# Attention forward and backward with grouped heads: K, V, dV and dK in nine shared places, and another order of the first three iterations

## The chip, the cores and the metric

The kernel runs on one core of one Trainium2 chip. The metric is the device time of one execution in microseconds (us): the median of three runs before the change is 684.23 us, the lowest 682.85, the highest 688.73. A core has these engines, each with its own instruction queue: TensorE (PE in the profile; its weight loads are PEld), VectorE (DVE), ScalarE (ACT), GpSimd (POOL) and SyncE (SP). Sixteen DMA engines move data between the device memory and the on-chip memory; in this kernel SP and POOL issue the transfers.

## The reference

For each of 32 batch entries there are 32 query heads with 4 queries each, 4 key/value heads with 2048 keys each, and a width of 128. Eight query heads share one key/value head. The forward pass and its gradients are wanted:

```python
k = jnp.repeat(k, rep, axis=1)          # rep = 32 // 4
v = jnp.repeat(v, rep, axis=1)
scores = jnp.einsum("bhqd,bhkd->bhqk", q, k) * D ** -0.5
p = softmax(scores, axis=-1)
out = jnp.einsum("bhqk,bhkd->bhqd", p, v)
# outputs: out, and the gradients of it for q, k, v with grad_out
```

All tensors are bf16. K, V, dK and dV are 2 MB each per batch entry, all else is small, so the kernel reads 136.31 MB and writes 136.31 MB.

## The kernel before

One iteration is one batch entry `b`. Its 32 x 4 = 128 query rows fill the 128 partitions: 32 rows (`G`) for each of 4 key/value heads (`NH`). The 2048 keys of a head are laid out as 128 partitions x 16 blocks (`C`), so K, V, dK and dV of one entry are each one tile of 128 partitions x 4 heads x 16 blocks x 128 numbers, 16 KB in each partition.

The work of an entry is cut into named pieces. `LK` and `LV` (lines 144 and 155) load K and V, one DMA of 512 KB for each head, issued by SP; every fourth `LK` also has the next four entries' q and grad_out loaded (`GROUP`). `QDT` transposes q and grad_out on TensorE; `KT0` to `KT7` and `VT0` to `VT7` transpose eight blocks of K or V each (eight matmuls against an identity, line 180) and VectorE copies the result out of PSUM (line 182). `Sa` and `Sb` are the scores of one half of the keys each (line 197) with the row maximum on VectorE (line 210); `EXa` and `EXb` are the exponentials on ScalarE (line 221). `NRM` makes the reciprocal sums on VectorE and, on GpSimd, the scaled query rows `dop` and `qp` (line 230). `ETa`, `ETb` transpose the exponentials (line 247). `O` multiplies them with V (line 263), and from the output comes the row term `delta`. `dPa`, `dPb` give `ds` (line 349), `dSTa`, `dSTb` transpose it, and `dQ` multiplies it with K (line 263). `dV0` to `dV7` and `dK0` to `dK7` are the outer products (line 306), two blocks of all heads each, copied out of PSUM by ScalarE (line 310). When all eight parts of a dV or dK are there, it is stored (line 132), by GpSimd until the last V has been asked for, then by SP; most stores are one DMA of 2 MB, dV of entry 0 and of every fourth entry is cut into three.

The order of all this is written out by hand. Inside `tc.manual_schedule()` (line 373) the pieces are emitted one after the other: `HEAD` for the first three iterations, `STEADY` (48 pieces, `+` and `-` marking a later or an earlier entry) for the iterations in the middle, `TAIL` for the last three. Each engine works through its own queue in that order, and an instruction waits on semaphores for what it needs. PSUM is one tile of eight banks, handed out by the class `Banks`, the bank released longest ago first.

The on-chip places of the four large tensors come from three pools: three buffers for K (`k_pool`, line 92), two for V (`v_pool`), four shared in turn by dV and dK (`out_pool`, line 100). A pool gives its buffers in rotation. So the load of K of entry b waits until `dQ` of entry b-3 has read the buffer, the load of V until `O` of entry b-2 has, and the first copy into a dV or dK until the store of the fourth output before it has landed.

Of the kernel before, what the change touches and what calls it, by code (L numbers as in the profile page):

```python
# [14 lines left out]


HEAD = """
LK@0 LV@0 QDT@0 KT4@0 KT6@0 KT2@0 KT0@0 KT3@0 KT5@0 KT1@0 KT7@0 LK@1 LV@1 VT2@0 Sa@0 Sb@0 VT5@0 VT3@0 EXb@0 VT4@0 EXa@0 VT0@0 QDT@1 KT4@1
KT6@1 KT2@1 KT0@1 NRM@0 ETb@0 ETa@0 VT7@0 KT3@1 VT6@0 VT1@0 dV7@0 O@0 dV5@0 dPb@0 dV1@0 KT5@1 KT1@1 dV3@0 dV6@0 dPa@0 KT7@1 dV2@0 LK@2 LV@2
VT2@1 dV4@0 Sa@1 dV0@0 Sb@1 dK7@0 VT5@1 VT3@1 EXb@1 dSTa@0 VT4@1 EXa@1 VT0@1 QDT@2 dSTb@0 KT4@2 dK1@0 dK6@0 KT6@2 KT2@2 KT0@2 NRM@1 dK0@0 dQ@0  # L20
dK3@0 dK5@0 dK2@0 ETb@1 ETa@1 VT7@1 KT3@2 VT6@1 VT1@1 dV7@1 dK4@0 O@1 dV5@1 dPb@1 dV1@1 KT5@2 KT1@2 dV3@1 dV6@1 dPa@1 KT7@2 dV2@1 LK@3 LV@3
VT2@2 dV4@1 Sa@2 dV0@1 Sb@2 dK7@1 VT5@2 VT3@2 EXb@2 dSTa@1 VT4@2 EXa@2 VT0@2 QDT@3 dSTb@1 KT4@3 dK1@1 dK6@1 KT6@3 KT2@3 KT0@3 NRM@2 dK0@1 dQ@1
dK3@1 dK5@1 dK2@1 ETb@2 ETa@2 VT7@2 KT3@3 VT6@2 VT1@2 dV7@2 dK4@1 O@2 dV5@2 dPb@2 dV1@2 KT5@3 KT1@3 dV3@2 dV6@2 dPa@2 KT7@3 dV2@2 LK@4 LV@4
VT2@3 dV4@2 Sa@3 dV0@2 Sb@3 dK7@2 VT5@3 VT3@3 EXb@3
"""
HEAD_ITERATIONS = 3

# [18 lines left out]
class Banks:  # L46


    def __init__(self, tile_):
        self.tile, self.clock = tile_, 0  # L50
        self.free_ = [True] * 8
        self.released = list(range(-8, 0))

    def take(self, n):
        best = None
        for i in range(0, 8, n):
            if all(self.free_[i:i + n]):
# [12 lines left out]
    def give(self, slot):  # L70
        for i in range(slot[0], slot[0] + slot[1]):
            self.free_[i] = True
            self.released[i] = self.clock
        self.clock += 1


@with_exitstack
def kernel(ctx: ExitStack, tc: tile.TileContext, q, k, v, grad_out, out_0, out_1, out_2, out_3):
    nc = tc.nc
# [9 lines left out]
    assert B % W == 0  # L89

    const = ctx.enter_context(tc.tile_pool(name="const", bufs=1))
    k_pool = ctx.enter_context(tc.tile_pool(name="kp", bufs=3))
    v_pool = ctx.enter_context(tc.tile_pool(name="vp", bufs=2))
    kt_pool = ctx.enter_context(tc.tile_pool(name="ktp", bufs=8))
    vt_pool = ctx.enter_context(tc.tile_pool(name="vtp", bufs=8))
    e_pool = ctx.enter_context(tc.tile_pool(name="ep", bufs=1))
    et_pool = ctx.enter_context(tc.tile_pool(name="etp", bufs=2))
    ds_pool = ctx.enter_context(tc.tile_pool(name="dsp", bufs=2))
    dst_pool = ctx.enter_context(tc.tile_pool(name="dstp", bufs=2))
    out_pool = ctx.enter_context(tc.tile_pool(name="outp", bufs=4))  # L100
    io_pool = ctx.enter_context(tc.tile_pool(name="iop", bufs=2))
    qd_pool = ctx.enter_context(tc.tile_pool(name="qdp", bufs=2))
    sm_pool = ctx.enter_context(tc.tile_pool(name="smp", bufs=3))
    ps_pool = ctx.enter_context(tc.tile_pool(name="ps", bufs=1, space=bass.MemoryType.PSUM))

    banks = Banks(ps_pool.tile([P, 8, 512], FP32, name="banks"))

    ident = const.tile([P, P], BF16, name="ident")
    make_identity(nc, ident[:])
# [20 lines left out]
    def store(**kw):  # L130

        (nc.sync if "v" in st.get(B - 1, {}) else nc.gpsimd).dma_start(**kw)  # L132
# [11 lines left out]
    def LK(b):  # L144
        S = st[b] = {}
        if b == 0:
            GROUP(0, nc.sync)
        S["q"], S["do"] = (x[:, b % W, :] for x in groups[b // W])
        if b % W == W - 1 and b + 1 < B:
            GROUP(b // W + 1, nc.gpsimd)  # L150
        S["k"] = k_pool.tile([P, NH, C, D], BF16, name="k_sb")
        for h in range(NH):
            nc.sync.dma_start(out=S["k"][:, h].rearrange("p c d -> p (c d)"), in_=k_v[b, h])  # L153

    def LV(b):
        S = st[b]
        S["v"] = v_pool.tile([P, NH, C, D], BF16, name="v_sb")
        for h in range(NH):
            nc.sync.dma_start(out=S["v"][:, h].rearrange("p c d -> p (c d)"), in_=v_v[b, h])

# [97 lines left out]
    def gathered(S, xt, kv):  # L258
        t = banks.take(1)
        ps = banks.ap(t)[:, 0, 0:D]  # L260
        for c in range(C):
            for h in range(NH):
                nc.tensor.matmul(  # L263
                    ps[G * h:G * h + G, :], lhsT=S[f"{xt}{c // 8}"][:, c % 8, G * h:G * h + G], rhs=S[kv][:, h, c, :],
                    start=(c == 0), stop=(c == C - 1), tile_position=(0, G * h),
                )
        return t, ps

    def O(b):
# [12 lines left out]
        nc.vector.tensor_tensor_reduce(  # L282
            out=junk[:], in0=o_sb, in1=S["do"], scale=1.0, scalar=0.0,
            op0=ALU.mult, op1=ALU.add, accum_out=S["delta"][:],
        )

    def dQ(b):
        S = st[b]
        t, ps = gathered(S, "dst", "k")
        dq_sb = io_pool.tile([P, D], BF16, name="dq_sb")  # L290
        nc.scalar.activation(out=dq_sb[:], in_=ps, func=ACT.Copy, scale=S["srinv"][:])
        banks.give(t)
        store(out=dq_f[b], in_=dq_sb[:])

    def outer(S, x, y, dst, name, i, b, copy):

        if name not in S:
            S[name + "left"] = 8
            S[name] = out_pool.tile([P, NH, C, D], BF16, name=name, tag="outp")
        t = banks.take(2)  # L300
        ps = banks.ap(t).rearrange("p a (j c d) -> p a j c d", j=2, c=2)
        for c in range(2):
# [7 lines left out]
        copy(  # L310
            out=S[name][:, :, 2 * i:2 * i + 2, :].rearrange("p h c d -> p h (c d)"),
            in_=banks.ap(t).rearrange("p a (j w) -> p (a j) w", j=2),
        )
        banks.give(t)
        S[name + "left"] -= 1
        if b == B - 1:

            half = f"{name}half{i // 4}"
            S[half] = S.get(half, 4) - 1
            if S[half] == 0:  # L320
                c = slice(8 * (i // 4), 8 * (i // 4) + 8)
                store(
                    out=dst[b].rearrange("p h (c d) -> p h c d", d=D)[:, :, c, :].rearrange("p h c d -> p h (c d)"),
                    in_=S[name][:, :, c, :].rearrange("p h c d -> p h (c d)"),
                )
        elif S[name + "left"] == 0:
            o = S.pop(name)[:].rearrange("p h c d -> p h (c d)")
            parts = [(slice(0, P), slice(0, NH))]

            if name == "dv" and b == 0:
                parts = [(slice(0, P), slice(0, 2)), (slice(0, 88), slice(2, 4)), (slice(88, P), slice(2, 4))]
            elif name == "dv" and b % 4 == 3:
                parts = [(slice(0, P), slice(0, 1)), (slice(0, 120), slice(1, 4)), (slice(120, P), slice(1, 4))]
            for r, h in parts:
                store(out=dst[b][r, h, :], in_=o[r, h])

    def dV(b, i, copy=nc.scalar.copy):
        outer(st[b], "e", "dop", dv_v, "dv", i, b, copy)  # L340
# [24 lines left out]
    for w in STEADY.split():  # L365
# [4 lines left out]
                break  # L370
        steady.append((w, ahead))

    with tc.manual_schedule():

        for w in HEAD.split():
            w, b = w.split("@")
            table[w](int(b))
        for it in range(HEAD_ITERATIONS, B - TAIL_ITERATIONS):
            for w, ahead in steady:
                if 0 <= it + ahead < B:  # L380
                    table[w](it + ahead)
        for w in TAIL.split():
            w, b = w.split("@")
            table[w](B + int(b))


# [28 lines left out]
```

## Time and profile before

| | |
|---|---|
| median of three runs | 684.23 us (682.85 to 688.73) |
| the profiled execution: its own time | 682.75 us |
| its span in the profile | 680.5 us |
| PE, DVE, ACT, POOL busy | 92%, 87%, 83%, 38% of the span |
| moved by DMA | 274.45 MB, mean 403 GB/s |
| DMA of K: issue to landing | 14.5 us (median), V 20.5 us |
| store of dK: issue to landing | 23.4 us (median), of an uncut dV 27.5 us |

The profile is one execution. The span is what the profiler sees, 2.25 us less than that execution's own time. Busy shares are means over the whole span; the share that counts is that of the stage looked at. The DMA share is the mean over the sixteen DMA engines. "<-" behind an idle time names what ended it. A queue's issue time (SPq, or POOL with DMA_DIRECT2D) says when the transfer was handed over, not when it moved.

### The profile page before, as it was taken

The page shows a single profiled execution, that of the slowest core. Times are in us where ns is not written, and L with a number is a line of the kernel's source. Part 1 is how long each engine was busy: PE and PEld are TensorE (multiplying, and loading weights), DVE is VectorE, ACT ScalarE, POOL GpSimd, SP SyncE. Part 2 cuts the span into 40 slices and gives each one's busy share as a digit, 9 for nine tenths or more (in the row PEclk, how much of TensorE's full clock was granted, in tenths as well). Part 3 has the DMA queues.
Part 4 walks back from the last instruction along what each step waited for, and adds up shares of the span by engine and source line. Part 5 has one row for each costly group of instructions (what it writes and reads, how often), then busy time and mean ns, then how long its engine had stood idle before and what let it go on. Part 6 is the DMA issues. An engine that isn't in the chain of part 4 may idle for free.

```text
span 680.5 us, 27999 instructions
## 1 busy us (share of the span) xinstructions
PE 623.7 (92%) x12352; PEld 449.1 (66%) x12352; DVE 594.5 (87%) x1003; ACT 563.3 (83%) x666; POOL 259.6 (38%) x436
## 2 busy tenths in 40 slices
PE   5899999999999999988999999899999999899984
PEld 4577766667776667765667766577666677566652
DVE  4999999899899889889888889789898898898895
ACT  0599898898888888888988888888888888896885
POOL 1254243534424454432535324353244542344310
PEclk9999999999999999999999999999999999999999
DMA  8989999999999999999999999999999999999998
GB/s 326 406 293 400 416 417 411 416 413 416 416 414 417 412 417 415 416 416 415 416 416 414 416 414 417 414 411 416 414 417 398 409 414 416 415 401 406 370 368 317
DMA packets 76483, 274.45 MB, mean 403 GB/s; under 512 B 8579, under 2 KB 8651, under 8 KB 76361
## 3 DMA queue, kind: packets, MB, share of 16 engines
q1 hardware_dynamic: 42185, 145.11, 53.2%
q0 software_dynamic: 34176, 127.55, 46.6%
q8 instruction: 96, 1.57, 0.8%
q14 instruction: 26, 0.21, 0.1%
HBM read 136.31 MB, written 136.31 MB: 401 GB/s over the span
## 4 chain that ended last, share of the span: by engine, by line
PE 53%; DMA 36%; DVE 4%; ACT 3%; issue 2%; SPq 1%; POOL 0%; ACTq 0%; DVEq 0%; POOLq 0%
DMA k_sb<-in_k_dram 35%; PE banks L180 22%; PE banks L306 14%; PE banks L263 8%; PE banks L197 5%; PE banks L247 5%; ACT dv L310 2%; DVE kt L182 1%; DMA v_sb<-in_v_dram 1%; SPq L153 1%; DVE dk L310 1%; DVE m L210 1%; PE banks L170 1%; DVE ds L349 1%; DVE vt L182 0%
## 5 line engine op out<-in xcount | busy, mean ns | idle before, releaser
L310 ACT CAST dv<-banks 128x1024 bf16<-128x1024 f32 x254 | 244.4, 1025 | 47.7 <-PE banks L306 47.1
L310 ACT CAST dk<-banks 128x1024 bf16<-128x1024 f32 x251 | 246.0, 1022 | 29.9 <-PE banks L306 26.9
L182 DVE COPY kt<-banks 128x1024 bf16<-128x1024 bf16 x256 | 165.1, 680 | 9.9 <-PE banks L180 9.8
L182 DVE COPY vt<-banks 128x1024 bf16<-128x1024 bf16 x256 | 166.4, 680 | 2.6 <-PE banks L180 2.0
L180 PE MATMUL banks<-ident,k_sb 128*128 128x128 bf16 x2048 | 148.0, 221 | 18.5 <-DMA k_sb<-in_k_dram 13.3
L230 POOL TENSOR_SCALAR dop<-do_sb,rinv 32x128 bf16<-32x128 bf16 x124 | 74.2, 598 | 220.6 <-PE banks L306 125.2
L180 PE MATMUL banks<-ident,v_sb 128*128 128x128 bf16 x2048 | 143.5, 219 | 12.4 <-ACT dv L310 8.8
L180 PEld LDWEIGHTS <-k_sb 128*128 128x128 bf16 x2048 | 120.7, 99 | 48.4 <-issue 31.8
L180 PEld LDWEIGHTS <-v_sb 128*128 128x128 bf16 x2048 | 121.3, 98 | 28.2 <-issue 26.2
L306 PE MATMUL banks<-dop,e 64*128 64x256 bf16 x1024 | 97.6, 273 | 7.0 <-issue 4.3
L349 DVE SCALAR_TENSOR_TENSOR ds<-banks,delta,e 128x1024 bf16<-128x1024 f32 x64 | 82.0, 1283 | 17.1 <-PE banks L197 17.0
L306 PE MATMUL banks<-qp,ds 64*128 64x256 bf16 x1024 | 87.0, 272 | 2.6 <-DVE dk L310 1.1
L132 POOL DMA_DIRECT2D out_dram<-dv x46 | 32.5, 708 | 139.9 <-ACT dv L310 133.5
L230 POOL TENSOR_SCALAR qp<-q_sb,srinv 32x128 bf16<-32x128 bf16 x128 | 77.9, 609 | 10.7
L221 ACT ACTIVATE e<-banks,negb 128x1024 bf16<-128x1024 f32 x64 | 70.7, 1111 | 11.4 <-DVE negb L213 11.4
L210 DVE TENSOR_REDUCE m<-banks 128x1 f32<-128x1024 f32 x64 | 75.2, 1215 | 1.7 <-PE banks L197 1.5
L306 PEld LDWEIGHTS <-e 64*128 64x128 bf16 x1024 | 34.0, 94 | 52.9 <-issue 36.6
L249 DVE COPY et<-banks 128x1024 bf16<-128x1024 bf16 x64 | 41.4, 685 | 27.1 <-PE banks L247 27.0
L306 PEld LDWEIGHTS <-ds 64*128 64x128 bf16 x1024 | 40.8, 94 | 30.8 <-ACT dv L310 12.6
L249 DVE COPY dst<-banks 128x1024 bf16<-128x1024 bf16 x64 | 43.4, 679 | 0.0
L197 PE MATMUL banks<-vt,qdt 128*32 128x512 bf16 x512 | 41.3, 384 | 1.8 <-issue 1.6
L197 PE MATMUL banks<-kt,qdt 128*32 128x512 bf16 x512 | 39.6, 384 | 0.7 <-DVE vt L182 0.3
(40 smaller groups left out, 460.1 us busy)
## 6 DMA issues: line engine op xcount, KB each, us to landing
k_sb<-in_k_dram SPq DMA_DIRECT2D x128, 512.0 KB, 14.5
v_sb<-in_v_dram SPq DMA_DIRECT2D x128, 512.0 KB, 20.5
out_dram<-dk POOLq DMA_DIRECT2D x29, 2048.0 KB, 23.4
out_dram<-dv POOLq DMA_DIRECT2D x22, 2048.0 KB, 27.5
out_dram<-dv POOLq DMA_DIRECT2D x7, 1440.0 KB, 27.2
out_dram<-dk SPq DMA_DIRECT2D x2, 2048.0 KB, 10.3
out_dram<-dv POOLq DMA_DIRECT2D x7, 512.0 KB, 20.4
out_dram<-dv SPq DMA_DIRECT2D x1, 2048.0 KB, 12.0
```

Of the source, the lines that this page charges most:

```text
L180: nc.tensor.transpose(out=ps[:, 4 * hh + j, :], in_=S[which][:, 2 * (i % 2) + hh, 4 * (i // 2) + j, :], identity=ident[:])
L182: nc.vector.tensor_copy(out=S[f"{which}t{i}"][:], in_=ps)
L197: nc.tensor.matmul(ps[G * h:G * h + G, a, :], lhsT=S["qdt"][:, col, G * h:G * h + G], rhs=xt[:, 4 * (h % 2):4 * (h % 2) + 4, :].rearrange( ...
L210: nc.vector.reduce_max(out=S["m"][:, i:i + 1], in_=S[f"s{i}"][1], axis=AX.X)
L221: nc.scalar.activation(out=S[f"e{i}"][:], in_=ps, func=ACT.Exp, bias=S["negb"][:], scale=scale, accum_out=S["l"][:, i:i + 1],)
L230: engine.tensor_scalar(out=t[r, h % 2, :], in0=src[r, :], scalar1=by[r, :], scalar2=None, op0=ALU.mult)
L247: nc.tensor.transpose(out=ps[:, u, :], in_=S[f"{src}{i}"][:, P * u:P * u + P], identity=ident[:])
L249: nc.vector.tensor_copy(out=S[f"{name}{i}"][:], in_=ps)
L263: nc.tensor.matmul(ps[G * h:G * h + G, :], lhsT=S[f"{xt}{c // 8}"][:, c % 8, G * h:G * h + G], rhs=S[kv][:, h, c, :], start=(c == 0), stop ...
L306: nc.tensor.matmul(ps[:, a, :, c, :], lhsT=S[f"{x}{i // 4}"][r, u:u + P], rhs=S[y][r, :, :], start=True, stop=True, tile_position=(2 * G * ...
L310: copy(out=S[name][:, :, 2 * i:2 * i + 2, :].rearrange("p h c d -> p h (c d)"), in_=banks.ap(t).rearrange("p a (j w) -> p (a j) w", j=2),)
L349: nc.vector.scalar_tensor_tensor(out=S[f"ds{i}"][:], in0=ps, scalar=S["delta"][:], in1=S[f"e{i}"][:], op0=ALU.subtract, op1=ALU.mult,)
```

## The change

The three pools `k_pool`, `v_pool` and `out_pool` go. In their stead one tile `places` has nine places of the same size, the same memory in all. A new class gives them out while the program is written: whoever asks gets, of the free places, the one with the oldest release. `LK` and `LV` take a place for K and V, the first part of a dV or dK takes one for the output. `O` gives V's place back, `dQ` gives K's, and the last part of a dV or dK gives its place back as stored, which adds 45 steps of the written order to its time of release. The diff shows `LK` for `LK` and `LV`, and `O` for `O` and `dQ`; then come two places in `outer`, at the first part of an output and behind its store. The waits themselves still follow from who last read or wrote the place. A step counter is moved on for each piece emitted (`run`).

`HEAD`, the order of the first three iterations, is replaced by another. It holds the same pieces; `STEADY` and `TAIL` are unchanged.

```diff
 HEAD = """
-LK@0 LV@0 QDT@0 KT4@0 KT6@0 KT2@0 KT0@0 KT3@0 KT5@0 KT1@0 KT7@0 LK@1 LV@1 VT2@0 Sa@0 Sb@0 VT5@0 VT3@0 EXb@0 VT4@0 EXa@0 VT0@0 QDT@1 KT4@1
-KT6@1 KT2@1 KT0@1 NRM@0 ETb@0 ETa@0 VT7@0 KT3@1 VT6@0 VT1@0 dV7@0 O@0 dV5@0 dPb@0 dV1@0 KT5@1 KT1@1 dV3@0 dV6@0 dPa@0 KT7@1 dV2@0 LK@2 LV@2
-VT2@1 dV4@0 Sa@1 dV0@0 Sb@1 dK7@0 VT5@1 VT3@1 EXb@1 dSTa@0 VT4@1 EXa@1 VT0@1 QDT@2 dSTb@0 KT4@2 dK1@0 dK6@0 KT6@2 KT2@2 KT0@2 NRM@1 dK0@0 dQ@0
...
+LK@0 KT2@0 KT6@0 QDT@0 KT4@0 KT0@0 KT5@0 KT7@0 KT1@0 LV@0 KT3@0 Sb@0 Sa@0 VT4@0 LK@1 VT2@0 EXa@0 QDT@1 VT7@0 EXb@0 VT1@0 NRM@0 ETa@0 LV@1
+KT4@1 ETb@0 VT0@0 VT6@0 VT3@0 VT5@0 LK@2 O@0 dV2@0 dV1@0 KT5@1 dV6@0 dPa@0 dV5@0 dPb@0 dV4@0 KT3@1 dV0@0 KT2@1 KT1@1 dV3@0 KT7@1 KT0@1 dV7@0
+KT6@1 dSTa@0 dK3@0 VT5@1 Sb@1 dK6@0 dK7@0 Sa@1 dSTb@0 EXb@1 VT7@1 KT0@2 EXa@1 VT1@1 dQ@0 LV@2 NRM@1 dK5@0 VT3@1 ETb@1 dK1@0 ETa@1 VT0@1 dK0@0
+VT2@1 dK4@0 VT4@1 VT6@1 O@1 dK2@0 KT4@2 dV5@1 dPb@1 KT5@2 KT2@2 dV7@1 KT7@2 KT1@2 dV3@1 QDT@2 dK6@1 KT3@2 VT6@2 dV4@1 VT7@2 dPa@1 dV6@1 LK@3
+dV1@1 dSTb@1 KT6@2 dV0@1 Sa@2 dV2@1 Sb@2 dK2@1 KT2@3 LV@3 dSTa@1 EXb@2 VT0@2 KT7@3 EXa@2 VT1@2 dK7@1 dQ@1 NRM@2 dK5@1 VT5@2 VT2@2 dK4@1 ETb@2
+ETa@2 dK3@1 KT5@3 VT3@2 dK1@1 KT6@3 dK0@1 KT1@3 VT4@2 QDT@3 LK@4 dV5@2 O@2 LV@4 dV4@2 dPb@2 KT0@3 dV6@2 KT3@3 dV3@2 KT4@3 dV7@2 VT2@3 dV0@2
+Sa@3 dPa@2 dV2@2 Sb@3 dK7@2 VT5@3 VT3@3 EXb@3 dV1@2
 """
...
+class Places:
+    N = 9
+    STORE = 45
+
+    def __init__(self, tile_):
+        self.tile, self.clock = tile_, 0
+        self.free_ = [True] * self.N
+        self.released = list(range(-100, -100 + self.N))
+
+    def take(self):
+        i = min((i for i in range(self.N) if self.free_[i]), key=lambda i: self.released[i])
+        self.free_[i] = False
+        return i
+
+    def give(self, i, stored=False):
+        self.free_[i] = True
+        self.released[i] = self.clock + (self.STORE if stored else 0)
...
-    k_pool = ctx.enter_context(tc.tile_pool(name="kp", bufs=3))
-    v_pool = ctx.enter_context(tc.tile_pool(name="vp", bufs=2))
+    place_pool = ctx.enter_context(tc.tile_pool(name="placep", bufs=1))
...
-    out_pool = ctx.enter_context(tc.tile_pool(name="outp", bufs=4))
...
+    places = Places(place_pool.tile([P, Places.N, NH, C, D], BF16, name="places"))
...
-        S["k"] = k_pool.tile([P, NH, C, D], BF16, name="k_sb")
+        S["kplace"] = places.take()
+        S["k"] = places.tile[:, S["kplace"]]
...
+        places.give(S["vplace"])
...
-            S[name] = out_pool.tile([P, NH, C, D], BF16, name=name, tag="outp")
+            S[name + "place"] = places.take()
+            S[name] = places.tile[:, S[name + "place"]]
...
+            places.give(S[name + "place"], stored=True)
...
+    def run(w, b):
+        places.clock += 1
+        table[w](b)
```

More of the change, by code (lines that the diff above doesn't have):

```diff
@@ L17 @@
 HEAD = """
-LK@0 LV@0 QDT@0 KT4@0 KT6@0 KT2@0 KT0@0 KT3@0 KT5@0 KT1@0 KT7@0 LK@1 LV@1 VT2@0 Sa@0 Sb@0 VT5@0 VT3@0 EXb@0 VT4@0 EXa@0 VT0@0 QDT@1 KT4@1
-KT6@1 KT2@1 KT0@1 NRM@0 ETb@0 ETa@0 VT7@0 KT3@1 VT6@0 VT1@0 dV7@0 O@0 dV5@0 dPb@0 dV1@0 KT5@1 KT1@1 dV3@0 dV6@0 dPa@0 KT7@1 dV2@0 LK@2 LV@2
-VT2@1 dV4@0 Sa@1 dV0@0 Sb@1 dK7@0 VT5@1 VT3@1 EXb@1 dSTa@0 VT4@1 EXa@1 VT0@1 QDT@2 dSTb@0 KT4@2 dK1@0 dK6@0 KT6@2 KT2@2 KT0@2 NRM@1 dK0@0 dQ@0
[L21 to L24, printed above, removed]
+LK@0 KT2@0 KT6@0 QDT@0 KT4@0 KT0@0 KT5@0 KT7@0 KT1@0 LV@0 KT3@0 Sb@0 Sa@0 VT4@0 LK@1 VT2@0 EXa@0 QDT@1 VT7@0 EXb@0 VT1@0 NRM@0 ETa@0 LV@1
[5 more added lines that the diff above has]
+Sa@3 dPa@2 dV2@2 Sb@3 dK7@2 VT5@3 VT3@3 EXb@3 dV1@2
 """
@@ L156, in LV @@
         S = st[b]
-        S["v"] = v_pool.tile([P, NH, C, D], BF16, name="v_sb")
+        S["vplace"] = places.take()
+        S["v"] = places.tile[:, S["vplace"]]
         for h in range(NH):
@@ L289, in dQ @@
         t, ps = gathered(S, "dst", "k")
+        places.give(S["kplace"])
         dq_sb = io_pool.tile([P, D], BF16, name="dq_sb")
@@ L376 @@
             w, b = w.split("@")
-            table[w](int(b))
+            run(w, int(b))
         for it in range(HEAD_ITERATIONS, B - TAIL_ITERATIONS):
@@ L380 @@
                 if 0 <= it + ahead < B:
-                    table[w](it + ahead)
+                    run(w, it + ahead)
         for w in TAIL.split():
             w, b = w.split("@")
-            table[w](B + int(b))
+            run(w, B + int(b))
 _INS = ['q', 'k', 'v', 'grad_out']
```

## The prediction

> **What bounds the kernel now.** I read the page's slices first, then the same stretches as windows, then the queues of the two engines that issue transfers.
>
> From the page (columns as its own legend has them):
>
> ```profile
> DMA  8989999999999999999999999999999999999998
> GB/s 326 406 293 400 416 417 411 416 413 416 416 414 417 412 417 415 416 416 415 416 416 414 416 414 417 414 411 416 414 417 398 409 414 416 415 401 406 370 368 317
> q1 hardware_dynamic: 42185, 145.11, 53.2%
> q0 software_dynamic: 34176, 127.55, 46.6%
> ```
>
> The 16 DMA engines are never idle, and from the fourth slice they move 411 to 417 GB/s. At 415 GB/s the 274.45 MB of the page need 661 us of the 680.5 us span. Loads (q1, issued by SP) and stores (q0, issued by POOL) share the engines about evenly. So bytes are the floor, and only stretches below 415 GB/s can be won. Where these lie, from the windows (length; busy time of PE, PEld, DVE, ACT, POOL; PE clock; DMA share; GB/s):
>
> ```profile
> 0.00:34.00 34.00, 23.27 (x364) 18.05 (x364) 23.55 (x40) 10.14 (x13) 7.21 (x21) 1.00 0.96 366
> 34.00:46.00 12.00, 11.48 (x238) 9.81 (x230) 11.14 (x21) 10.32 (x15) 5.16 (x9) 1.00 0.78 254
> 46.00:60.00 14.00, 13.55 (x254) 9.50 (x250) 13.53 (x23) 13.19 (x16) 6.59 (x10) 1.00 1.01 389
> 60.00:81.20 21.20, 20.91 (x459) 15.14 (x458) 19.73 (x34) 19.10 (x23) 7.25 (x12) 1.00 1.02 413
> 261.00:595.00 334.00, 309.56 (x6188) 222.61 (x6176) 292.76 (x498) 284.49 (x337) 134.10 (x220) 1.00 1.03 414
> 640.00:680.50 40.50, 29.06 (x595) 18.63 (x592) 30.97 (x48) 28.51 (x34) 4.86 (x9) 0.97 0.86 335
> ```
>
> Time lost against 415 GB/s is length times (1 - rate/415): 4.0 us before 34 (first loads arriving), **4.7 us in 34 to 46**, 0.9 us in 46 to 60, nothing to speak of in the middle, 7.8 us after 640. The hole at 34 is explained by SP's issues and POOL's stores:
>
> ```profile
> 27.86 1.75 SPq L159 DMA_DIRECT2D v_sb<-in_v_dram  x4
> 42.13 3.13 SPq L153 DMA_DIRECT2D k_sb<-in_k_dram  x4
> 47.23 1.79 SPq L159 DMA_DIRECT2D v_sb<-in_v_dram  x4
> 61.53 3.49 SPq L153 DMA_DIRECT2D k_sb<-in_k_dram  x4
> 66.84 1.86 SPq L159 DMA_DIRECT2D v_sb<-in_v_dram  x4
> 81.22 1.84 SPq L153 DMA_DIRECT2D k_sb<-in_k_dram  x4
> ```
>
> ```profile
> 35.36 2.33 POOL L132 DMA_DIRECT2D out_dram<-dv  x3 [5.95 <-ACT dv L310]
> 49.13 0.78 POOL L132 DMA_DIRECT2D out_dram<-dk  x1
> 54.75 0.75 POOL L132 DMA_DIRECT2D out_dram<-dv  x1 [2.62 <-ACT dv L310]
> 68.61 0.76 POOL L132 DMA_DIRECT2D out_dram<-dk  x1
> 74.35 0.75 POOL L132 DMA_DIRECT2D out_dram<-dv  x1 [4.98 <-ACT dv L310]
> ```
>
> V of 2 lands at 35.1 (the chain shows 28.71 plus 6.37 for it); K of 3 is issued at 42.13, because its buffer is that of K of 0, which dQ of 0 reads until about 42.1. Between them only dV of 0 moves, in three pieces. Meanwhile the output buffers stand empty.
>
> What an early byte is worth shows in the chain of waits of the middle:
>
> ```profile
> 344.67 16.47 DMA k_sb<-in_k_dram
> 361.14 0.05 issue
> 361.19 0.40 PE banks L180 x4
> ```
>
> From 261 on this comes back in most iterations: K is released by dQ, takes 16 to 17 us behind the earlier V and beside the stores, and PE waits. Until 261 PE sets the pace, 20.0 us an iteration (61.53 to 261.19 in ten). So bytes moved earlier push the start of the DMA-bound part back and end the kernel earlier, microsecond for microsecond, until the about 12 us that the waits for K cost after 261 (16 periods of 20.87 us in place of some 20.1) are used up.
>
> **The change, part by part.** I followed the nine places through the written order by hand, "first free, oldest release first", 45 steps added for a stored place.
>
> *Head, loads.* K0 V0 K1 V1 K2 V2 get fresh places. V2 no longer waits for O of 0 (27.86), but up to 34 the engines move 383 to 416 GB/s anyway: gain under 0.2 us, counted as nothing. K3 takes K0's place (after dQ of 0, as now), V3 takes V1's (after O of 1, as now), K4 takes dV0's and V4 dK0's, each after that store has landed. dV0, dK0 and dV1 take fresh places, dK1 takes V0's.
>
> *Head, order.* VectorE sets the pace from 9 to 60 (of 20 us in 40 to 60 it works 18.71). Transposed copies run 0.6 us apart (four in 2.47). Ahead of dQ of 0 stand 32 such copies in place of 37, one QDT (0.28) and one NRM (0.31) fewer: 3.0 + 0.6 = 3.6 us. ScalarE's queue grows there (eight dV copies in a row at 1.02, then three dK and two EX of 1.3), which gives some back: I take 3 us, K3 at about 39. Ahead of O of 1 stand four copies and a QDT fewer: 2.7 us, V3 at 44.5. K4 comes right behind it, at about 46.5, 15 us earlier than now, since dV0 lands some 10 us after its issue (the page's row of its 320 KB piece is 10.0). The last dV of 0 needs four copies fewer ahead of its start, but O of 0 now stands there (0.73): 1.7 us by DVE, and ScalarE's eight copies, 8.2 us, follow as now. By DVE it is 1.7 us, by ScalarE's count 1; I take 1, the store at 34.4. dK0's store moves from 49.1 to about 46.8, dV1's to 55.5, dK1's to 66.5, dV2's from 74.35 to 76.8 (a dK copy and one EX more stand ahead of it on ScalarE). At dQ of 2 both orders have done the same work on every engine, so K5 stays at 81.2.
>
> The ledger: from 34.4 to 39 only dV0 moves, at about 272 GB/s (the mean of 225, 244 and 348 in 34 to 40 now): 4.6 x (1 - 272/415) = 1.6 us lost. From 39 something is always queued: K3 and the rest of dV0 to 46.6, then V3, K4, dK0, dV1, V4 (10.5 MB and small ones, 26.5 us) to 73.1, dK1 (66.5) to 78.2, dV2 (76.8) beyond 81.2. The hole costs 1.6 in place of 4.7 + 0.9, so 4.0 us are won, less 0.1 of bends: **3.9 us**. Bounds: all 5.6 us if dV0 hides too; nothing if new waits for banks in the head hold PE 4 us longer. No row shows these waits in this order; the nearest, PE waiting for the dV copies, is 8.8 us in 27 waits, 0.33 each, so a few would cost 1 to 2 us. I take 0 for them and keep 2.
>
> At this place the Trainium skill speaks against the change: "DMA: Bandwidth & Descriptors", section "Issuing engines are not separate DMA queues", has all transfers run on the same 16 engines and interleave, whoever started them. By that alone an early load only displaces a store, and the sum would be 0; the trace agrees where the engines are full (415 GB/s), not in 34 to 46 (254).
>
> *Middle.* K of b+2 goes on taking the place of K of b-1, and dV that of dV two iterations back, as now. Two trade: dK takes V's place just freed by O (no wait), and V of b+2 takes that of dK of b-2, so it waits for a store to land. In the profile, V is issued at 349.40; that dK's store was issued at 330.30, and such stores land after 23.4 us (page, median), so at 353.7: V is 4.3 us late. SP's queue holds only the next K behind it, at 364.95. V's bytes could not move before K has landed (361.1) in any case, so the wait is covered with 7 us to spare: 0. If that cover is gone, V's lateness reaches K's chain.
>
> *Dependencies, clock, tail.* Waits drawn by region, not by tile, cost nothing: now already the first four K transposes start at 7.04 on one head's load, the rest at 8.31. The tail keeps its order, and its last places are free long before they are asked for: 0.
>
> Sum: 682.75 us of the profiled execution (span 680.5 and 2.25 around it) less 3.9 gives 678.85. That execution lies 1.5 us under the median of the runs, 684.23, so the forecast on the median's footing is 684.23 - 3.9 = **680.3 us**.
>
> **Rivals.**
> - *The hole only moves* (0.24). K4 and V4 are in early, but K5 still waits for dQ of 2 at 81.2; if dV2's store comes later than 78, the engines run dry there, or bank waits hold the head. For: dV2's store is 2.5 us later by my count. Against: the queue reaches to 78.2. The whole 3.9 given back: 684.2. The page's rule above ends here too.
> - *V gated by dK's store* (0.14), slower. Place: the middle, when a dK store takes over 31 us from issue to landing (361.1 - 330.3), so that V cannot follow K at once. For: dV stores take up to 29.5 us. Against: dK stores take at most 25.5. Price: half a microsecond in each of 25 iterations less the head's 3.9, 684.2 + 12.5 - 3.9 = 693.
> - *All K waits go* (0.07): if places freed earlier let the queues run closer to the ceiling, PE's pace holds to the end: 684.2 - 12 = 672. Against: 261 to 595 already moves 414 GB/s.
> - *It doesn't do what it says* (0.03): waits drawn on the whole shared tile put each load behind running reads. Two 16 us loads an iteration in series with 20 us of PE would give above 1,000 us. The 7.04 start speaks against it.
>
> **How the numbers follow.** The forecast has 0.52. A change under 1% (6.8 us) is about what a measurement of this kernel can tell from none. Faster by over 1% needs 677.4: the K-wait rival and the forecast's luckiest part, 0.07 + 0.07 = 0.14. Slower, over 691: most of the V rival, the last one and a long-stalled head, 0.12 + 0.03 + 0.04 = 0.19. The same: 0.67. The range: down to 684.23 - 5.6 less 1.4 (the lowest run shown), 677, widened to 676 towards the third rival; up to the rival without gain plus a head 2 us longer plus the 4.5 us to the highest run shown: 691.
>
> **What would show it.** Right: SP issues V2 well before 27, K3 near 39, K4 near 46.5; the rate in 34 to 60 rises to about 390; 60 to 81 stays near 413; PE's regular waits for K start some seven iterations later (3.9 over 0.55 us, the gap of 20.55 us for an iteration's 8.5 MB to 20.0). Wrong: a slice under 400 GB/s between 60 and 100, SP waiting for dK's store until K has landed, or PE idle for banks in the head.

## The result, and the profile after

The change is slower by half a per cent: the median goes from 685.89 us (681.36 to 690.30, 20 runs) to **688.63 us** (685.49 to 692.85, 20 runs), ratio 1.0050, 95% interval 1.0031 to 1.0070. A second series of the same kernel gave 1.0057 (1.0038 to 1.0076). The forecast was a ratio of 0.994. The time lies inside the forecast range, on the wrong side of no change.

The profiled execution of the changed kernel is the slowest of its 20 runs: 692.85 us, span 690.7. The two profiles lie 10.2 us apart, the medians 2.7. So the profiles say where time can go; how much it costs is read from the ratios. (The ratios are estimated from the undisturbed runs and are not simply the quotients of the medians beside them.)

The page's slices after the change, 17.3 us each:

```profile
DMA  9999999999999999999999999999999999999988
GB/s 337 406 306 403 404 383 355 359 404 416 415 359 417 413 417 416 414 415 413 417 415 416 416 415 416 415 407 415 415 416 404 405 404 415 417 376 409 389 342 316
```

The third slice holds the old hole: 306 GB/s, before 293. New are slices six to eight, 86 to 138 us, at 383, 355 and 359, where the kernel before moved 411 to 417. The DMA share is nine tenths or more there: the engines count as busy and move less. The same stretches as windows of the changed kernel (length; busy PE, PEld, DVE, ACT, POOL; PE clock; DMA share; GB/s):

```profile
34.00:46.00 12.00, 11.66 (x274) 8.56 (x271) 11.38 (x20) 9.24 (x12) 6.75 (x11) 1.00 0.88 278
46.00:60.00 14.00, 13.48 (x210) 8.84 (x212) 13.64 (x23) 12.27 (x14) 5.16 (x7) 1.00 1.02 389
60.00:81.20 21.20, 19.72 (x389) 13.60 (x381) 19.30 (x33) 17.70 (x23) 7.15 (x12) 1.00 1.01 403
81.20:145.00 63.80, 55.39 (x1100) 39.14 (x1099) 50.46 (x86) 50.60 (x59) 25.01 (x42) 0.97 0.99 372
145.00:261.00 116.00, 112.28 (x2274) 82.28 (x2271) 105.49 (x183) 102.60 (x123) 48.71 (x81) 1.00 1.02 407
```

Two things are to be seen. From 34 to 46 the rate rose only from 254 to 278. From 81.2 to 145 it is 372 in place of 414, and PE is busy for 55.39 of 63.80 us: it is not full either. Where PE stood idle between 60 and 145, from its waits in the changed kernel (what ended them: us in total, times, longest):

```profile
PE banks L286 <- issue: 3.9, 2, 2.4
PE banks L332 <- issue: 3.3, 2, 2.4
PE banks L332 <- DVE ds L376: 1.3, 1, 1.3
PE banks L220 <- issue: 0.7, 1, 0.7
```

"issue" means that no awaited event shows. Such waits make 7.9 us here; in the kernel before they make 0.8 between 60 and 145. The last section says what they are. SP's issues of the changed kernel (start, length, line, transfer):

```profile
39.78 4.43 SPq L175 DMA_DIRECT2D places<-in_k_dram  x4
45.65 1.81 SPq L182 DMA_DIRECT2D places<-in_v_dram  x4
47.99 3.88 SPq L175 DMA_DIRECT2D places<-in_k_dram  x4
64.72 2.07 SPq L182 DMA_DIRECT2D places<-in_v_dram  x4
84.02 2.93 SPq L175 DMA_DIRECT2D places<-in_k_dram  x4
87.05 2.68 SPq L182 DMA_DIRECT2D places<-in_v_dram  x4
106.00 5.59 SPq L175 DMA_DIRECT2D places<-in_k_dram  x4
111.71 2.15 SPq L182 DMA_DIRECT2D places<-in_v_dram  x4
131.36 1.99 SPq L175 DMA_DIRECT2D places<-in_k_dram  x4
```

K of 5, which `dQ` of 2 releases, is issued at 84.02 in place of 81.22; K of 6 at 106.00 in place of 100.78; K of 7 at 131.36 in place of 120.96. After that the distance hardly changes: K of 13 comes 11.1 us later than before, K of 30 10.4, K of 31 10.2, and from K of 31 to the end both spans take 61.6 to 61.7 us. **The ten microseconds of these two profiles arise ahead of the eighth iteration and are carried to the end.**

The ledger of bytes says the same of where the time went. The time lost against 415 GB/s was summed as in the prediction over the windows 12 to 34, 34 to 60, 60 to 145, 145 to 261 and 261 to 600. It is 7.0 us before and 16.1 after; of the difference, 7.0 us lie in 60 to 145 and 2.2 in 145 to 261, while 34 to 60 gained 0.8. In all fourteen profiles of this study span less lost time is 672.6 to 678.0 us, while the spans run from 680.1 to 691.2. Since every kernel moves the same bytes, this is close to bookkeeping: it adds only that the losses outside the windows, ahead of 12 and behind 600 us, differ by no more than these 5.4 us, which is still twice the difference of the medians. The ledger shows in which stretch a profile lost its time and not why. The forecast was wrong about which microseconds would be lost.

### The profile page after: what moved, and what is told of

Read it like the earlier page. It is cut to its first block, busy times and chain, and to the rows that moved or that the text cites. A ratio compares the mean times of both kernels' runs of the same rounds, so it can differ in the third digit from the quotient of the medians.

```text
span 690.7 us, 28192 instructions
## 1 busy us (share of the span) xinstructions
PE 629.8 (91%) x12352; PEld 452.3 (65%) x12352; DVE 596.3 (86%) x1003; ACT 563.2 (82%) x666; POOL 259.2 (38%) x436
## 3 DMA queue, kind: packets, MB, share of 16 engines
q0 software_dynamic: 34176, 127.55, 46.5%
## 4 chain that ended last, share of the span: by engine, by line
PE 63%; DMA 17%; ACT 9%; DVE 5%; issue 4%; SPq 0%; ACTq 0%; DVEq 0%
PE banks L203 28%; DMA places<-in_k_dram 15%; PE banks L332 15%; ACT places L336 8%; PE banks L286 8%; PE banks L270 7%; PE banks L220 4%; DMA places<-in_v_dram 1%; DVE m L233 1%; DVE vt L205 1%; DVE ds L376 1%; PE banks L193 1%; DVE places L336 1%; DVE kt L205 1%; SPq L182 0%
## 5 line engine op out<-in xcount | busy, mean ns | idle before, releaser
L336 ACT CAST places<-banks 128x1024 bf16<-128x1024 f32 x505 | 480.7, 1023 | 87.7 <-PE banks L332 83.0
L203 PE MATMUL banks<-ident,places 128*128 128x128 bf16 x4096 | 286.2, 222 | 32.5 <-DMA places<-in_k_dram 11.2
L203 PEld LDWEIGHTS <-places 128*128 128x128 bf16 x4096 | 242.8, 99 | 79.8 <-issue 64.0
L153 POOL DMA_DIRECT2D out_dram<-places x75 | 54.9, 733 | 167.3 <-ACT places L336 161.9
L332 PE MATMUL banks<-qp,ds 64*128 64x256 bf16 x1024 | 88.5, 273 | 3.7 <-DVE ds L376 1.6
L220 PEld LDWEIGHTS <-qdt 128*32 128x32 bf16 x1024 | 17.6, 94 | 34.6 <-issue 33.4
L270 PE MATMUL banks<-ident,ds 128*128 128x128 bf16 x512 | 38.9, 219 | 0.9 <-ACT places L336 0.9
L286 PE MATMUL banks<-places,et 128*32 128x128 bf16 x2048 | 35.1, 220 | 3.9 <-issue 3.9
```

The costliest lines, as they stand in the source:

```text
L203: nc.tensor.transpose(out=ps[:, 4 * hh + j, :], in_=S[which][:, 2 * (i % 2) + hh, 4 * (i // 2) + j, :], identity=ident[:])
L220: nc.tensor.matmul(ps[G * h:G * h + G, a, :], lhsT=S["qdt"][:, col, G * h:G * h + G], rhs=xt[:, 4 * (h % 2):4 * (h % 2) + 4, :].rearrange( ...
L270: nc.tensor.transpose(out=ps[:, u, :], in_=S[f"{src}{i}"][:, P * u:P * u + P], identity=ident[:])
L286: nc.tensor.matmul(ps[G * h:G * h + G, :], lhsT=S[f"{xt}{c // 8}"][:, c % 8, G * h:G * h + G], rhs=S[kv][:, h, c, :], start=(c == 0), stop ...
L332: nc.tensor.matmul(ps[:, a, :, c, :], lhsT=S[f"{x}{i // 4}"][r, u:u + P], rhs=S[y][r, :, :], start=True, stop=True, tile_position=(2 * G * ...
L336: copy(out=S[name][:, :, 2 * i:2 * i + 2, :].rearrange("p h c d -> p h (c d)"), in_=banks.ap(t).rearrange("p a (j w) -> p (a j) w", j=2),)
```

## The experiments

Times are medians, ratios are to the kernel before on the same chip, with 95% intervals. "Lost" is that ledger's sum for 34 to 60 and for 60 to 145 us; K5 and K7 are the issues of K of entries 5 and 7; all four are from the one profiled execution.

| kernel | median us | ratio (interval) | lost 34-60 | lost 60-145 | K5 | K7 |
|---|---|---|---|---|---|---|
| before | 685.1 to 685.9 | 1 | 5.6 | 0.2 | 81.22 | 120.96 |
| the change | 688.63 | 1.0050 (1.0031-1.0070) | 4.8 | 7.2 | 84.02 | 131.36 |
| the change, second series | 688.65 | 1.0057 (1.0038-1.0076) | 5.3 | 4.7 | 85.05 | 129.26 |
| places, old order | 685.50 | 1.0003 (0.9973-1.0032) | 1.3 | 4.1 | 80.20 | 120.03 |
| pools, new order | 687.43 | 1.0009 (0.9984-1.0034) | 5.9 | 4.5 | 85.33 | 128.13 |
| change, V in O's place | 688.02 | 1.0023 (0.9999-1.0048) | 3.1 | 4.7 | 82.86 | 123.25 |
| change, K4 and V4 late | 686.96 | 1.0035 (1.0003-1.0068) | 3.1 | 4.7 | 82.28 | 123.26 |
| places, old order, V in O's place | 684.01 | 0.9982 (0.9964-1.0000) | 1.3 | 4.1 | 80.63 | 120.12 |
| the same once more | 684.33 | 0.9989 (0.9967-1.0012) | 1.1 | 3.7 | 79.96 | 120.06 |
| change, dP of 2 earlier | 688.89 | 1.0049 (1.0022-1.0076) | 4.4 | 4.7 | 83.85 | 128.07 |
| before, PE 3 us later | 692.52 | 1.0084 (1.0053-1.0116) | 6.2 | 4.5 | 84.86 | 130.08 |
| change, less PE work | 688.59 | 1.0030 (1.0005-1.0056) | 5.1 | 6.6 | 83.73 | 130.52 |
| before, less PE work | 684.79 | 0.9994 (0.9975-1.0013) | 5.5 | 0.2 | 80.58 | 119.93 |
| change, filler for PE | 688.95 | 1.0058 (1.0037-1.0079) | 3.4 | 4.1 | 82.38 | 124.90 |

### Each half alone

Places with the old order: the diff of the change without its `HEAD`.

```diff
 HEAD = """
-LK@0 KT2@0 KT6@0 QDT@0 ...
+LK@0 LV@0 QDT@0 KT4@0 ...
```

> The shared places with the old order of the first three iterations. By hand through the written order: K3 now takes V0's place, free since O of 0 at 27.8, so it follows V2 at once instead of waiting for dQ of 0 at 42; V3 takes K0's place (42), K4 K1's (61.5), V4 dK0's once that is stored (about 65), and V of b+2 that of dK of b-2 from there on. Theory A (the new order costs the time, the places cost nothing): 0 to 3 us faster than the kernel before, since the hole at 34 to 46 closes in part. Theory B (V's wait for a dK store costs the time, in every iteration): slower than before by 2 to 7 us. Theory C (K4 and V4 loaded 15 us early leave the load queue empty and then come back to back with K5 and V5): within 2 us of before, since K4 is not early here.

Measured: 1.0003. The hole is gone here, and the bytes are lost again behind it. Windows of this kernel, columns as above:

```profile
34.00:46.00 12.00, 11.75 (x268) 10.22 (x271) 11.14 (x21) 10.31 (x14) 5.94 (x10) 1.00 1.03 404
46.00:60.00 14.00, 13.55 (x251) 9.30 (x241) 13.37 (x23) 12.90 (x17) 5.94 (x9) 1.00 1.02 388
60.00:81.20 21.20, 20.75 (x460) 15.44 (x449) 19.42 (x35) 19.35 (x24) 7.35 (x13) 1.00 0.99 381
81.20:145.00 63.80, 61.66 (x1250) 45.26 (x1250) 58.00 (x99) 56.41 (x67) 28.97 (x49) 1.00 1.02 399
```

404 GB/s stand where the kernel before moves 254, and 381 and 399 where it moves 413 and 414: 4.3 us are won up to 60, 3.9 are lost again up to 145. SP's issues of the same kernel say how the hole was filled:

```profile
22.63 4.17 SPq L182 DMA_DIRECT2D places<-in_v_dram  x4
27.82 4.12 SPq L175 DMA_DIRECT2D places<-in_k_dram  x4
41.24 4.70 SPq L182 DMA_DIRECT2D places<-in_v_dram  x4
```

`LK` of 3 stands at the same point in both orders, as the 95th and the 96th piece, behind `dQ` of 0. What differs is where dK of 1 starts. With the old order its first part is the 102nd piece, so K of 3 finds the place that `O` of 0 has given back and is issued at 27.82. In the changed kernel `dK6` of 1, the 89th piece, takes that place first; K of 3 is left with the place of K of 0, waits for `dQ` of 0, and is issued at 39.78. So of the two halves the places fill the hole, and with the new order most of it stays open. (The new order with that one place kept for K of 3 was not run.)

The new order with the three pools as they were: the diff of the change without `Places`.

> The three pools as before, with the new order of the first three iterations. A: slower than before by 3 to 6 us, as much as the change or more, with dQ of 2 ending 2 to 3 us later than in the profile before. B: no slower than before, 0 to 2 us faster, since K3 is issued near 39 in place of 42. C: the same as B.

Measured: 1.0009 (0.9984 to 1.0034); its median, 687.43, is 2.3 us above that of before, so a slowdown of that size is neither shown nor excluded. K5 is at 85.33, K7 at 128.13, and 81.2 to 145 moves 389 GB/s. The late K comes with the order, not with the places. A dip behind 60 shows with either half (381 and 399 in the other).

Each half alone stays within the measurement. Together they give 1.0050 and 1.0057, whose intervals lie above no change. Whether the halves add up or make each other worse, intervals of this width do not say.

The change once more, in a second series:

> The changed kernel once more, for a second trace (the first one, 692.85 us, was the slowest of its 20 runs) and as the yardstick of this set. Both theories: 2 to 4 us slower than before; SP's issue of K5 at 82.5 to 84, against 81.2 before.

1.0057: the slowdown stands. The profile of this series is a typical one, 688.65 us against a median of 688.65: K5 at 85.05, and 3.7 us of "issue" waits between 60 and 145.

### V behind the store of dK

```diff
-        S["vplace"] = places.take()
+        S["vplace"] = places.take(st[b - 2]["vplace"] if b >= 5 else None)
```

(`take` gives the place asked for if it is free.)

> The change, but from entry 5 on V takes the place that O of two entries before has just given back, as in the kernel before; dK then takes that of dK two entries before. SP no longer waits for a dK store in the middle. A: like the change, 2 to 4 us slower than before. B: 1 to 4 us faster than before. C: like the change in 80 to 140, so 1 to 4 us slower.

In the changed kernel SP waits for stores with V's load queued behind them (us in total, times, longest):

```profile
SPq L182 <- DMA out_dram<-places: 104.4, 21, 12.8
```

This wait is gone here but for one of 12.3 us, that of V of 4, and the ratio falls from 1.0050 and 1.0057 to 1.0023. The same edit on places with the old order:

> The shared places with the old order of the first three iterations, and from entry 5 on V takes the place that O of two entries before has just given back, so that no load waits for a dK store in the middle. If V's wait for a store costs anything, this is 1 to 2 us faster than the same without it (which was 1.0003 of before): 0.997 to 0.9985 of before. If it costs nothing: 1.000.

0.9982, against 1.0003 with the wait; and once more:

> Nine places, the old written order, V in the place that O left: the kernel that measured 0.9982 (0.9964 to 1.0000), once more. If places without V's wait for dK's store are worth about a microsecond: 683.5 to 684.5, 0.997 to 0.999. If that was chance: 1.000.

0.9989. Taking V's wait away moved the ratio down in both pairs, by 0.001 to 0.003 or about 1 to 2 us. No single pair of intervals is disjoint, so the size is an estimate. This kernel is faster than the change, and it has the lowest medians of the table, 684.0 and 684.3; against the kernel before it is not told apart from no change.

### K and V of entry 4 late

K of 4 and V of 4 were given places that come free later, so that the bytes are asked for no earlier than before.

```diff
-        S["kplace"] = places.take()
+        S["kplace"] = places.take(st[1]["kplace"] if b == 4 else None)
...
-        S["vplace"] = places.take()
+        S["vplace"] = places.take(st[2]["vplace"] if b == 4 else None)
```

> The change, but K4 takes the place of K1 and V4 that of V2, as in the kernel before, so neither is loaded early; K0 to V3 stay as in the change, and V waits for a dK store from entry 5 on. A: slower than before by 3 to 6 us. B: slower by 3 to 6 us. C: 0 to 2 us either side of before, and the slices from 80 to 140 stay above 410 GB/s.

1.0035, and 390 GB/s between 81.2 and 145, as in the kernel with V in O's place (389), which loads entry 4 early. The theory that the loads of entry 4 were moved ahead and only left their gap behind 81 falls for this order: with them put back the gap stays.

### TensorE at the end of the head

In every profile with the new order K of 5 is late, 82.3 to 85.3, and never with the old one alone, 80.0 to 81.2. The windows up to that issue, before and after:

```profile
0.00:81.22 81.22, 69.23 (x1300) 52.51 (x1302) 67.98 (x115) 52.77 (x63) 26.20 (x51) 1.00 0.96 366
0.00:84.02 84.02, 72.00 (x1300) 53.09 (x1302) 69.77 (x117) 53.14 (x63) 26.27 (x51) 0.98 0.97 371
```

TensorE has run 1300 matmuls in both, and takes 2.8 us longer. Is this lateness the cause of the lost time? Four kernels move TensorE's work at that point.

One PE wait of 1.3 us for `ds` at 75 us can be taken away by writing `dPa` of 2 ahead of `Sa` of 3:

```diff
-Sa@3 dPa@2 dV2@2 Sb@3 ...
+dPa@2 Sa@3 dV2@2 Sb@3 ...
```

> The changed kernel with one pair of pieces exchanged: dPa of 2 ahead of Sa of 3. In the trace of every kernel with the new order TensorE waits 1.2 to 1.3 us near 75 for ds of entry 2, which VectorE makes behind the row maximum of Sa of 3. Theory P (TensorE's lateness at the end of the head is passed on to the end, one for one): this wait goes, K5 is issued 1.2 us earlier than in the change run beside it, and the end comes 1 us earlier. Theory M (the bytes moved in the head set the end, a late TensorE is absorbed): the same time as the change.

1.0049. The wait for `ds` shrank to 0.16, and PE waited 1.21 us at 77.85 for a copy of V's transposes on VectorE instead: the wait moved from one of VectorE's results to another. K5 came at 83.85, 0.2 us ahead of the first profile of the change and 1.2 ahead of the second, and the time did not move.

The kernel before, with 48 transposes that nothing reads ahead of `dQ` of 2, 2.8 us of PE in its trace:

```diff
+        if b == 2:
+            t, ps = bank16()
+            for u in range(48):
+                nc.tensor.transpose(out=ps[:, u % 8, :], in_=ident[:], identity=ident[:])
+            banks.give(t)
```

> The kernel before with 48 further transposes of the identity, which nobody reads, ahead of dQ of 2: about 3 us more of TensorE at 80, by the 0.54 to 0.61 us of eight in the trace. No load or store of the first three iterations is otherwise touched. P: 2.5 to 3.5 us slower than before. M: 0 to 1 us slower, since at 81 the DMA queues still hold some 5 us of work, which goes on while TensorE is late.

1.0084 (1.0053 to 1.0116): 5.8 us, by the interval 3.6 to 8.0, for 2.8 us of work. Pools, order and loads are those of before. SP's issues of K:

```profile
84.86 1.76 SPq L153 DMA_DIRECT2D k_sb<-in_k_dram  x4
...
105.22 6.67 SPq L153 DMA_DIRECT2D k_sb<-in_k_dram  x4
...
130.08 2.09 SPq L153 DMA_DIRECT2D k_sb<-in_k_dram  x4
```

These are close to the times of the changed kernel (84.02, 106.00, 131.36) in a kernel that has none of the change, with 6.4 us of "issue" waits of PE between 60 and 145 (the change: 7.9 and 3.7 in its two profiles) and 4.5 us lost there (7.2 and 4.7). **Work added to TensorE ahead of `dQ` of 2 is enough to make the picture, and it costs 1.3 to 2.8 times its length.** Two things limit this. The profile also has the halved clock at 20 to 24 that the next section is about, and K of 4 is already 0.8 us late there, at 62.31. And added matmuls shift TensorE's program against the blocks in which it is fetched (last section), in every later iteration. The profiles with 24 matmuls fewer show 18 "issue" waits each between 20 and 660 us (7.5 and 11.1 us), those with 28 and 48 more 34 and 29 (23.9 and 22.7), those with the number unchanged 24 to 34 (12.4 to 23.6). The runs that add or leave out matmuls change both things, and none keeps them apart.

The other direction: 24 transposes and three copies of V of 2 left out, in the change and in the kernel before.

```diff
+        if b == 2 and i in (1, 5, 2):
+            st[b][f"vt{i}"] = st[b]["vt0"]
+            return
         turned(st[b], "v", vt_pool, i)
```

(In the kernel before, pieces 5, 3 and 4 stand back for piece 2.)

> The change, with 24 of the transposes of V of entry 2 and three of its eight copies left out (three of the transposed pieces stand in for others, so the softmax gradient of that entry is computed from wrong columns; every load and store stays). That is some 1.6 us of TensorE (32 transposes took 2.17 us) and 1.9 us of VectorE (a copy takes 0.64) less before dQ of entry 2. Theory P (what of the head is late on TensorE at dQ of entry 2 is kept to the end): K5 is issued at 82.5 to 83.5 instead of 84.0 to 85.1, K7 some 2 us or more earlier than 129 to 131, and the time falls from 688.65 by 1.6 us or more, to 685.5 to 687, 1.000 to 1.003 of before. Theory M (the bytes moved early set the end): loads and stores are the same, so the time stays at 688 to 689, 1.005. The wait for ds at 75 may take some of it back: then K5 moves by under 0.7 us and the time by no more than that.

> The kernel before, with the same 24 transposes and three copies of entry 2 left out. Theory P: the old order too ends earlier by what TensorE has less to do ahead of dQ of entry 2: K5 at 79.5 to 80 instead of 81.2, time 682.5 to 684, 0.995 to 0.998 of before. Theory M, and also if the hole at 34 to 46 sets the end in this kernel: 1.000. Three more microseconds of TensorE work at this place cost 5.8; if the answer is one-sided (late costs, early gains nothing), this run gives 1.000 and TensorE is no bound in the old order.

In the change K5 moved by only 0.3 to 1.3 us against its two profiles, as the wait for `ds` stayed at 1.3 us; 1.0030 says little. In the kernel before, K5 and K7 came 0.6 and 1.0 us earlier and the time stayed, 0.9994. A gain of 0.6 to 1.0 us would be 0.9985 to 0.9991, inside the interval of 0.9975 to 1.0013. So it is not shown that the answer is one-sided; a gain of 2 us, twice what K7 won, would be 0.9971 and lies outside.

### The clock

In five of the eight profiles with the new order the granted clock halves at 20 to 24 (0.57 to 0.62), behind the stretch where PE waits 1.2 and 1.4 us for VectorE's copies of V. Of those with the old order only the one with added PE work shows it (0.57). Filler work was put there:

```diff
+        if b == 1:
+            for u in range(20):
+                nc.tensor.transpose(out=ps[:, 2 + u % 6, :], in_=ident[:], identity=ident[:])
...
-        for hh in range(2):
+        for hh in (0, 1, 0, 1) if S is st[0] and (which, i) == ("v", 1) else (0, 1):
```

> The change with 28 transposes more (20 in the bank of QDT of entry 1 that nothing reads, 8 of VT1 of entry 0 a second time), put where TensorE stands idle for 1.2 and 1.4 us at 17 to 20 us. Theory C (the idle stretch halves the clock at 20 to 24, and that makes K5 1 to 2 us late): the granted clock stays near 1 at 20 to 24, K5 at 82.3 to 83, K7 at 123 to 126, and the time falls by 1 to 2.5 us, to 686 to 687.5, 1.001 to 1.004. Rival: the clock drop takes nothing that lasts, since VectorE is what the head waits for later: the drop goes and the time stays at 688 to 689, 1.005. If the filler holds VectorE up: K5 later than 85, over 1.006.

The windows 16 to 24 of the change, then of this kernel:

```profile
16.00:20.00 4.00, 1.46 (x23) 1.17 (x21) 3.66 (x7) 2.79 (x4) 0.00 (x0) 0.98 1.03 407
20.00:24.00 4.00, 4.00 (x46) 4.00 (x45) 2.88 (x7) 0.79 (x2) 2.39 (x4) 0.59 1.03 411
```

```profile
16.00:20.00 4.00, 3.02 (x52) 2.73 (x50) 3.30 (x7) 3.16 (x4) 0.00 (x0) 1.00 1.04 411
20.00:24.00 4.00, 3.97 (x117) 3.58 (x115) 3.51 (x8) 0.42 (x2) 2.61 (x5) 1.00 1.03 410
```

The granted clock stays at 1.00, K5 comes at 82.38 and K7 at 124.90, as the clock theory said. The time did not move: 1.0058 (1.0037 to 1.0079). Nine of its 11 runs had a mean clock of 0.997 or more, higher than the other kernels, and lay at 687.8 to 690.0. **The clock drop goes with a later K5 in the profiles, but without it the change is as slow.** What took this kernel's gain at K7 back in its typical runs is not known, and the 28 added matmuls shift the program here too: its profiled execution, at 694.27 us the slowest of its 11, shows one "issue" wait of 2.7 us at 194 us, which a typical run need not have.

## Why the prediction was wrong

- **"At dQ of 2 both orders have done the same work on every engine, so K5 stays at 81.2"**: this step failed. The amount of work is the same, the time it takes is not: K5 comes 1.1 to 4.1 us late. With the new order PE waits 1.2 and 1.4 us at 17 to 20 for VectorE's copies of V and 1.3 us at 75 for `ds`, where the working took 0 for such waits. But the old order waits elsewhere: up to the issue of K5 PE runs the same 1300 matmuls and is idle for 12.0 us in both profiles, in the changed kernel 5.0 of them for other engines and 6.8 for loads, before 4.1 and 7.9. The 2.8 us between 81.22 and 84.02 lie in PE's busy time, 72.00 us in place of 69.23. The halved clock at 20 accounts for some 1.7 of them, an estimate from 3.41 us at half speed. In the two profiles with the new order and neither drop nor filler, K5 is 1.1 and 1.6 us late, with PE busy for 69.8 us and idle for 12.4 and 13.0. What such lateness costs later was nowhere in the working; the run with 2.8 us of extra work measured 5.8. The forecast's own sign of being wrong, a slice under 400 GB/s between 60 and 100, came true with the 383 of slice six.
- **"From 39 something is always queued"**, hence a hole of 1.6 in place of 5.6 us: this failed too. Something was queued, but not enough: from 38 to 44 the changed kernel moves 295, 225 and 214 GB/s in steps of 2 us, with the rest of dV of 0 and, from 39.78, K of 3 in flight. 34 to 60 lost 4.8 us. The forecast priced the rate of a thin queue at 272 only until 39 and at 415 from the moment K of 3 was issued.
- **The times in the head** were close: store of dV0 34.4 (measured 34.29), K3 39 (39.78), V3 44.5 (45.65), K4 46.5 (47.99), dK0 46.8 (48.36), dV1 55.5 (57.41), dK1 66.5 (68.36), dV2 76.8 (79.86). All but the first came late, from 0.8 us at K3 to 3.1 at dV2.
- **V's wait for dK's store, 0 with 7 us to spare**: too low, by the estimate above. Removing it brought about 1 to 2 us in two pairs, whose intervals overlap. The rival made of it named the right place, but with 13 us far too high a price.
- **"Microsecond for microsecond"**: right as bookkeeping, to within the 5.4 us by which the fourteen profiles scatter. It was applied to bytes moved before 60 and not to what the engines could be given between 60 and 145.
- **The rival "the hole only moves"** is what places with the old order do: 4.3 us won, 3.9 lost again, 1.0003. The changed kernel does worse than that rival, since its order fills little of the hole and is late besides.
- **The page's rule beside that rival**, the Trainium skill's "DMA: Bandwidth & Descriptors", section "Issuing engines are not separate DMA queues", has all transfers run on the same 16 engines, whoever started them; the forecast drew from it that an early load only displaces a store. In the kernel with places and the old order the sum came out as by that rule, a gain near 0. But the rates of 381 and 399 behind 60 point to engines with too little to do rather than to displaced stores.
- **Waits for K start later**: in the first profile they nearly went. PE waits for K 3.5 us in 4 times between 261 and 600, before 9.6 us in 13; in the second profile of the change it is 6.3 in 8. No gain came of it: the periods of K behind 261 stayed at 20.9 us, and "issue" waits rose from 8.9 to 12.6 us in the first profile.
- **The tail at 0**: right, 61.6 and 61.7 us from K of 31 to the end.

What is shown: the new order makes K5 late (eight profiles with it, against five with the old order and no work added), and work added to TensorE at this point slows the old kernel with like marks. What is argued: that 1.1 to 1.6 us, the lateness without a clock drop, at a factor of two makes the 2.7 us between the medians. Against a fixed factor speaks the new order with the three pools: K5 comes 4.1 us late there and the time is 1.0009, at most 1.0034. What stays open: how the 2.7 us divide between this lateness and V's wait for stores, what the shifted program does in the runs with added work, why the engines move 327 to 342 GB/s at nearly full share when few transfers are in flight, and what takes the filler kernel's gain back.

## What to carry to other kernels

When a kernel runs at the DMA ceiling with TensorE's pace next to it, a hole in the transfers is only worth filling if something is left to move later: for each stretch, list what can have been issued, and price a thin queue at the rate the trace shows for one, not at the ceiling. Two written orders that hold the same work by a given point need not reach it at the same time, so follow the waits of the engine that sets the pace up to where the head hands over, because lateness there can be kept. And try the halves of such a change apart: here the memory scheme with the old order and without its extra wait was faster than the whole change, though not told apart from the kernel before.

## What the runs showed of the hardware

**TensorE waits for its own program.** The "issue" waits of PE are late code. The page lists a DMA queue for it, here that of the changed kernel (97 packets where 28 or 48 matmuls were added, 96 in all others):

```profile
q8 instruction: 96, 1.57, 0.8%
```

96 packets of 16 KB serve 12352 matmuls and as many weight loads, so one for every 128 pairs. In all fourteen profiles, of four different numbers of matmuls and both orders, every such wait between 20 and 660 us falls where the matmul's number in the program, counted from 0 and divided by 128, leaves 95. In the single records of the trace these waits end 1.2 to 1.7 us after such a packet has landed (median 1.4). The timeline of the changed kernel has it in the middle of `O`, between matmuls of one gather that wait for nothing:

```profile
110.01 0.29 PE L286 MATMUL banks<-places,et 128*32 128x128 bf16 x7
112.73 1.00 PE L286 MATMUL banks<-places,et 128*32 128x128 bf16 x57 [2.42 <-issue]
```

The kernel before waits at the same matmul, for 0.33:

```profile
104.75 0.29 PE L263 MATMUL banks<-v_sb,et 128*32 128x128 bf16 x7
105.38 1.00 PE L263 MATMUL banks<-v_sb,et 128*32 128x128 bf16 x57 [0.33 <-issue]
```

A code packet starts a median of 3.3 to 3.7 us after PE has crossed the boundary before it, and takes 0.95; with the 1.4 that is about 6 us, longer than PE needs for 128 pairs where its work is dense (about 5.0 to 5.6). So it is on the edge in every iteration, and what delays the packet stops PE. Over all profiles, from 20 to 600 us, the packet started later than 4.2 us in 8 of 861 cases where the DMA moved over 412 GB/s in the 4 us behind the crossing, and in 17 of 63 where it moved less than 370. The wait of 2.42 is such a case: the boundary was crossed at 105.04, and the queues of the changed kernel from 105.1 to 110.2 and from 110.2 to 112.7 (queue: packets, MB, share) show no code until 110.2, with the total at 335 GB/s in the first stretch:

```profile
q0 software_dynamic: 427, 1.49, 88.4%
q1 hardware_dynamic: 57, 0.22, 12.7%
```

```profile
q1 hardware_dynamic: 191, 0.72, 79.3%
q0 software_dynamic: 35, 0.05, 8.2%
q8 instruction: 1, 0.02, 2.3%
```

From 20 us to 660 "issue" waits of PE make 12.9 us in the profile before and 23.6 after. The Trainium skill, "Runtime: NRT & Kernel Launch", section "Instruction fetch mechanics", says that code comes in blocks of 16 KiB, 256 instructions, over the sequencer's own DMA queue, and that a crossing is mostly hidden. The trace agrees with the block (128 pairs); hidden it is not here, with 12.9 and 23.6 us of waits.

**Full share is not full rate.** With few transfers in flight the sixteen engines showed a share of 0.97 to 0.98 and moved 327 to 342 GB/s (106 to 118 in the changed kernel). The typical 4 KB packet still took 0.159 us there, but the mean was 0.19 in place of 0.16 (300 to 320 us): 8% of the packets took over 0.32 us, in place of 0.3%. A share near 1 in the page's slices therefore does not say that the stretch is at the ceiling; the GB/s line does.

**The clock gate.** From the start to 660 us the fourteen profiles show 23 stretches at half the clock, 21 of 3.41 us and two of 6.83. In the 4 us ahead of each PE was busy for 0.4 to 2.3 us: at 20 us behind the stretch in the head, later behind a wait of 1.7 to 4.2 us for code or for K. After the same stretch in the head, with PE busy for 1.46 and 1.48 us of the four from 16 to 20, two of the profiles with the new order show no drop. The Trainium skill, "TensorE: Matmul & The Clock Gate", part 1 on the clock gate, has a free-running window of about 3.4 us, so that the moment of a change depends on where in the window the work falls, and varies between runs. The trace agrees with the length and with the variation.
